# Moving stores, a split, six additions and the inverse in the second half of a fused attention and two-layer network kernel

## The chip, the cores and the metric

The kernel runs on one core of a Trainium2 chip. The metric is the device time of one execution in microseconds (us). Times of the kernel before: 1921.9 us is the median of three runs (1918.7, 1921.9, 1922.95).

## The reference

```python
def _moe2_ref(x, w_in, w_out, a, b):
    h = x @ w_in                                   # 4608 x 512 times 512 x 2048
    P = a[0] + a[1] * h + a[2] * h2 + a[3] * h3    # h2 = h*h, h3 = h2*h
    Q = 1.0 + np.abs(b[0]) * np.abs(h) + np.abs(b[1]) * h2
    g = P / (Q + 1e-06)
    return (g @ w_out).astype(np.float32)          # 2048 x 512
...
x = attention(q, k, v)            # pooled keys and values
x = _moe_ref(x, ...)              # a gated network, 512 -> 1536 -> 512
return _moe2_ref(x, ...)
```

Attention and the first network fill the first 1025 us of the span and are not touched. The change lies in the second network (`_moe2_ref`), which the kernel calls its second phase.

## The kernel before

The 4608 tokens are nine blocks of 512 (`j` = 0 to 8). The 2048 columns of `h` are cut into 16 slices of 128 (`f`), two slices make a quad pair `q` (0 to 7). Products are of float32 accuracy: every operand is split into a high part (rounded copy, ScalarE) and a low part (the rest, a subtraction), and `mm3` (L257) does three matmuls for each product.

**Stage A** (1025 to 1270 us) takes blocks 0 to 2 plainly: 24 sets `n`, one for each (j, q). Set `n` has 24 matmuls for `h` (a PSUM tile `h` with two buffers), then one or two calls of `out2()`. `out2()` is 12 matmuls that add one slice of `g @ w_out` for an earlier set into four PSUM banks `acco`. Class `Units` works on a set's `h`: on ScalarE `a_square` (squares L1123, absolute value L1124), `a_line` (L1127), `a_log` (logarithm L1131, exponential L1132). On VectorE `v_under` (L1136), `v_over` (L1140, L1141; both read PSUM) and `v_inverse` (L1145, L1146), after which `quotient` (L1152) writes `g`. The tiles `w4`, `t4` and `ln4` have two halves, used by even and odd sets in turn. In between, sets 1 to 16 prepare sums of the input weights for stage B: on odd sets `i_sums` (L1211 to L1218: two additions of 128x512, four of 128x256, on GpSimd), on even sets `i_parts` splits them (`ip`). Sets 3 to 6 and 11 to 14 split the next block's input (`z`), sets 18 to 21 do a sum of stage B's inputs on VectorE (`token_sum`), sets 20 to 23 split such a sum (`token_part2`).

**Stage B** (1270 to 1859 us) takes blocks 3 to 8 two at a time, in 24 rounds `m` (three pairs of blocks times eight q). Such a round uses seven products of 6 matmuls instead of eight (`product2`, with sums and differences of blocks), and four calls of `out2()`; 90 matmuls in all. In order on TensorE: a11, out2 number 1, s1, s2, out2 number 2, a12 and s4, s3, out2 number 3, a22, out2 number 4. After a11 ScalarE copies bank `a` into bank `b` (L1351, the mark of a round below); s1 goes to bank `c` of the same PSUM tile `hb` and so starts behind that copy. After s1 ScalarE copies `c` out (`cq`, L1354). Then unit `one` of the round goes through `Units` after s4, unit `two` after a22; the second half of unit `two` (logarithm, inverse, quotient) is done in the next round. Rounds 7, 8, 15 and 16 also split inputs of the next pair (`z`).

`next_split()` gives the two halves of the split of a finished `g` for `out2()`: `high` on ScalarE (L1175) and `low` on GpSimd (L1178), both 128x1024, into a tile `gt` with two buffers. A round makes two splits: the first behind unit `one`'s `a_line`, the second behind unit `two`'s. In the end, what is left of `out2()` runs by itself (the tail, with the low parts on VectorE).

**Block end.** When slice f = 15 of a block is done, `out2()` at once copies the four banks `acco` to tiles `ob` (L1200, ScalarE, two buffers) and stores each (L1202) by a DMA on SyncE's queue. Six block ends fall into stage B, always behind out2 number 1 of a round (rounds 1, 5, 9, 13, 17, 21), so that the copies stand on ScalarE ahead of unit two's `a_log` and of the copy L1351. One falls into stage A (set 13), two into the tail.

Of the kernel before, what the change touches and what calls it, by code (L numbers as in the profile page):

```python
# [10 lines left out]
F32 = mybir.dt.float32  # L11
F32R = mybir.dt.float32r
U32 = mybir.dt.uint32
AF = mybir.ActivationFunctionType
ALU = mybir.AluOpType
# [4 lines left out]
P = 128  # L20
# [43 lines left out]
def attention_gated_rational(  # L64
# [1041 lines left out]
    with tc.tile_pool(name="p2", bufs=1, reuse_waits="tile") as p2:  # L1106
# [43 lines left out]
        def quotient(j, q, t, e):  # L1150
            g = stash[j, q] = wslot(f"g{j}_{q}", (P, 2, BLK), F32)
            nc.vector.scalar_tensor_tensor(g, t, neg[:, 0:1], e, op0=ALU.add, op1=ALU.mult)  # L1152
# [26 lines left out]
                outs.extend(((j, 2 * q + s), gt[:, :, s, :]) for s in range(2))  # L1179
            return high, low  # L1180

        def out2():

            for fn in waiting:
                fn()
            waiting.clear()
            if not outs:
                return
            (j, f), gt = outs.pop(0)
            if f == 0:  # L1190
                accs[j] = alloc_acc(f"o{j}")
            w = o2_t.pop(0)
            for i in range(4):
                mm3(accs[j][i], [(gt, slice(i * P, (i + 1) * P), w, full)], first=f == 0, last=f == NF2 - 1)
            o2_load()
            if f == NF2 - 1:
                acc = accs.pop(j)
                for i in range(4):
                    ob = p2.tile([P, DM], F32, tag="ob", name=f"ob{j}_{i}", bufs=2)
                    nc.scalar.activation(ob, acc[i], AF.Copy)  # L1200
                    r0 = j * BLK + i * P
                    nc.sync.dma_start(out[r0 : r0 + P, :], ob)  # L1202


        sums2 = {}
# [1 line left out]
        def i_sums(k):  # L1207
            r = wslot(f"ir{k}", (P, 2, 2, QUART), F32)
            for i in range(2):
                w = W2[f"i2_{2 * k + i}"]  # L1210
                nc.gpsimd.tensor_tensor(  # L1211
                    r[:, i].rearrange("p h c -> p (h c)"), f32(w[:, 0, :]), f32(w[:, 1, :]), op=ALU.add
                )
            t = sums2[k] = wslot(f"is{k}", (P, 4, QUART), F32)
            nc.gpsimd.tensor_tensor(t[:, 0], r[:, 1, 0], r[:, 1, 1], op=ALU.add)
            nc.gpsimd.tensor_tensor(t[:, 1], t[:, 0], r[:, 0, 0], op=ALU.subtract)
            nc.gpsimd.tensor_tensor(t[:, 2], r[:, 0, 0], r[:, 1, 0], op=ALU.subtract)
            nc.gpsimd.tensor_tensor(t[:, 3], r[:, 0, 1], t[:, 1], op=ALU.subtract)  # L1218

        def i_parts(k):  # L1220
            t = sums2.pop(k)
# [65 lines left out]
        for n, (j, q) in enumerate(sets):  # L1287
            if j + 1 < PLAIN and q == 1:
                raws[j + 1] = keep.tile([P, KT, BLK], F32, tag="xraw", name=f"yraw{j + 1}")
                nc.sync.dma_start(raws[j + 1], y_dram[j + 1])  # L1290
            if j + 1 < PLAIN and q == 3:
                xs[j + 1], cv = convert_x(halves(raws.pop(j + 1)), f"z{j + 1}", True)
                xs["cv"] = cv
            if j == PLAIN - 1 and q == 1:
                raw_load(0)
            h = ps_h.tile([P, 2, BLK], F32, tag="h", name=f"h2_{j}_{q}")
            for i in range(2):
                mm3(h[:, i, :], [(W2[f"i2_{2 * q + i}"], slice(kk * P, (kk + 1) * P), xs[j][kk], full) for kk in range(KT)])
                if j == PLAIN - 1:
                    W2.pop(f"i2_{2 * q + i}")  # L1300
            u = Units(h, n % 2)
            for _ in range(1 if n % 4 else 2):
                out2()
            u.a_square()
            u.a_line()
            cut = next_split() if len(outs) < 2 else None
            if cut:
                cut[0]()
            u.v_under()
            u.v_over()  # L1310
            if cut:
                cut[1]()
            u.a_log()
            if xs.get("cv"):
                xs["cv"].pop(0)()
            u.v_inverse()
            quotient(j, q, t4[:, n % 2], w4[:, n % 2])
            k, r = divmod(n - 1, 2)
            if 0 <= k < NQ:
                (i_parts if r else i_sums)(k)  # L1320
            if 1 <= k < NQ + 1 and not r:
                i_store(k - 1)
            if j == PLAIN - 1:
                if 2 <= q < 6:
                    token_sum(0, q - 2)
                if q >= 4:
                    token_part2(0, ("b11", "t1", "t2", "b21")[q - 4])
                if q == 6:
                    stream2(0)
            if q == NQ - 1:  # L1330
                xs.pop(j)


        nm = len(PAIRS2) * NQ
        old = None
        for m in range(nm):
# [15 lines left out]
            product2(c, m, "s1", "t1", True)  # L1352
            cq = p2.tile([P, BLK], F32, tag="cq", name=f"cq2_{m}")
            nc.scalar.activation(cq, c, AF.Copy)  # L1354
            product2(a, m, "s2", "t2")
            if old:
                old[1].v_inverse()
# [18 lines left out]
            product2(a, m, "s3", "t3")  # L1376
            one.a_square()
            one.a_line()
            cut = next_split()
            if cut:  # L1380
                cut[0]()
            nc.vector.tensor_tensor(h22, cq, a, op=ALU.add)  # L1382
            one.v_under()
            one.v_over()
            if cut:
                cut[1]()
            one.a_log()
            out2()
            product2(a, m, "a22", "t4")
# [82 lines left out]
```

## Time and profile before

| what | value |
|---|---|
| median of three runs | 1921.9 us |
| the profiled execution | 1922.85 us |
| its span (first to last instruction) | 1921.1 us |
| TensorE busy, share of the span | 1761.4 us, 92% |
| VectorE busy | 1362.1 us, 71% |
| ScalarE busy | 1105.2 us, 58% |
| GpSimd busy | 578.5 us, 30% |
| mean granted TensorE clock | 0.976 of full |
| stores of the result | 36 of 256 KB |

TensorE is the engine with most work, and matmuls are pipelined, so its busy share overstates how near it is to its peak. The table averages over stages with different limits. What the change is worth has to be read stage by stage, from what each engine waits for.

### The profile page before, as it was taken

Reading aid. Unit: us, or ns where it says so; the run is one execution under the profiler, and the core shown is the slowest. Engines: PE = TensorE matmul, PEld = TensorE weight load, DVE = VectorE, ACT = ScalarE, POOL = GpSimd, SP = SyncE. Lnnn points to the kernel's source line nnn. Section 1 sums busy time; section 2 is a strip of 40 time slices with the busy share of each in tenths; the row PEclk is TensorE's granted clock in tenths of the full one; section 3 lists DMA queues with packets and bytes.
Section 4 is the critical chain, followed back from the end, with each engine's and each line's share of the span. In section 5 each row is a group of like instructions: output and inputs, shape, how many; then the busy total and the mean of one; then the engine's idle time right before and its main releaser. Section 6 shows DMA issues by size and latency. Waiting matters only on the chain.

```text
span 1921.1 us, 23468 instructions
## 1 busy us (share of the span) xinstructions
PE 1761.4 (92%) x8068; PEld 1409.6 (73%) x8068; DVE 1362.1 (71%) x1852; ACT 1105.2 (58%) x1636; POOL 578.5 (30%) x603
## 2 busy tenths in 40 slices
PE   6889999999999999999999899977989798989898
PEld 5667777777787787878887677766767676767677
DVE  7996665566777666457777999985869586957671
ACT  5685455556656655345555666665657465756562
POOL 2344545424352542200003485211212121212120
PEclk9999999999999999999999999988999899989999
DMA  7522756579998889999353244344545555454535
GB/s 253 204 98 80 235 176 212 181 254 351 364 326 293 315 312 311 346 369 316 135 197 136 105 152 167 134 163 167 194 160 186 189 171 180 165 186 164 186 121 175
DMA packets 201670, 404.80 MB, mean 211 GB/s; under 512 B 16208, under 2 KB 88528, under 8 KB 200912
## 3 DMA queue, kind: packets, MB, share of 16 engines
q1 hardware_dynamic: 200832, 402.98, 60.4%
q8 instruction: 64, 1.05, 0.2%
q14 instruction: 54, 0.44, 0.1%
q10 hardware_dynamic: 720, 0.33, 0.1%
HBM read 305.73 MB, written 97.52 MB: 210 GB/s over the span
## 4 chain that ended last, share of the span: by engine, by line
PE 41%; DVE 10%; ACT 4%; DMA 4%; POOL 3%; issue 2%; SPq 0%; POOLq 0%; ACTq 0%; DVEq 0%
PE acco L257 14%; PE hb L257 6%; PE ya L1082 5%; PE ha L257 5%; PE ca L257 4%; POOL gt L1178 3%; PE yc L1082 3%; DVE w L1136 3%; PE cc L257 2%; DMA out<-ob 2%; DVE w L1146 2%; DVE w L1145 2%; PE yb L1082 1%; DVE t L1141 1%; DVE t L1140 1%
## 5 line engine op out<-in xcount | busy, mean ns | idle before, releaser
L257 PE MATMUL acco<-wo,gt 128*128 128x512 f32 x1728 | 421.0, 392 | 26.7 <-POOL gt L1178 25.4
L257 PEld LDWEIGHTS acco<-wo,gt 128*128 128x128 f32 x1728 | 323.1, 188 | 106.2 <-POOL gt L1178 37.0
L1178 POOL TENSOR_TENSOR gt<-g,gt 128x1024 fp32r<-128x1024 f32 x63 | 157.9, 2506 | 777.2 <-ACT gt L1175 740.5
L257 PE MATMUL h<-z,wi 128*128 128x512 f32 x576 | 142.5, 405 | 18.9 <-DVE t L1141 17.5
L257 PEld LDWEIGHTS h<-z,wi 128*128 128x128 f32 x576 | 111.4, 196 | 48.6 <-issue 16.1
L1145 DVE SCALAR_TENSOR_TENSOR w<-w,ln 128x1024 f32<-128x1024 f32 x72 | 98.7, 1371 | 60.5 <-ACT ln L1132 60.5
L1131 ACT ACTIVATE ln<-w 128x1024 f32<-128x1024 f32 x72 | 76.4, 1062 | 74.5 <-DVE w L1136 74.3
L257 PE MATMUL vp<-x,wv 128*128 128x512 f32 x432 | 111.0, 404 | 5.9 <-DVE wv L150 5.9
L1136 DVE SCALAR_TENSOR_TENSOR w<-sq,neg,w 128x1024 f32<-128x1024 f32 x72 | 110.0, 1528 | 8.8 <-ACT w L1124 8.7
L257 PE MATMUL gp<-x,wg 128*128 128x512 f32 x432 | 109.4, 400 | 2.5 <-DVE wg L150 2.5
L257 PE MATMUL acc<-ht,wo 128*128 128x512 f32 x432 | 106.8, 396 | 0.0
L1123 ACT ACTIVATE sq<-hb 128x1024 f32<-128x1024 f32 x24 | 24.7, 1029 | 138.7 <-PE hb L257 138.7
L257 PEld LDWEIGHTS vp<-x,wv 128*128 128x128 f32 x432 | 80.5, 191 | 26.0 <-DVE wv L150 8.5
L257 PEld LDWEIGHTS gp<-x,wg 128*128 128x128 f32 x432 | 79.4, 188 | 23.4 <-DVE wg L150 4.7
L1175 ACT ACTIVATE gt<-g 128x1024 fp32r<-128x1024 f32 x72 | 76.5, 1063 | 34.0 <-PE acco L257 25.6
L1146 DVE SCALAR_TENSOR_TENSOR w<-w,ln 128x1024 f32<-128x1024 f32 x72 | 93.8, 1303 | 2.5
L1152 DVE SCALAR_TENSOR_TENSOR g<-t,neg,w 128x1024 f32<-128x1024 f32 x72 | 94.2, 1336 | 1.1
L257 PEld LDWEIGHTS acc<-ht,wo 128*128 128x128 f32 x432 | 80.4, 188 | 18.3
L1132 ACT ACTIVATE ln<-ln,lnb 128x1024 f32<-128x1024 f32 x72 | 83.0, 1152 | 2.3
L118 POOL TENSOR_TENSOR rawo<-rawo 128x256 uint32<-128x256 uint32 (+1 forms) x41 | 31.2, 760 | 133.0 <-DVE rawo L115 63.0
L1382 DVE TENSOR_TENSOR ha<-cq,ha 128x512 f32<-128x512 f32 x24 | 16.7, 696 | 63.9 <-PE ha L257 63.7
L257 PE MATMUL ca<-x1t,sw 128*128 128x512 f32 x216 | 57.6, 401 | 2.4 <-DVE x1t L95 2.1
(318 smaller groups left out, 4046.0 us busy)
## 6 DMA issues: line engine op xcount, KB each, us to landing
wo<-o_parts SPq DMA_DIRECT2D x144, 512.0 KB, 3.7
sw<-sd SPq DMA_DIRECT2D x72, 512.0 KB, 7.5
iw<-si SPq DMA_DIRECT2D x48, 512.0 KB, 7.6
sw<-wd SPq DMA_DIRECT2D x36, 512.0 KB, 5.8
h<-hq SPq DMA_DIRECT2D x36, 512.0 KB, 7.0
sd<-sp SPq DMA_DIRECT2D x24, 512.0 KB, 4.1
iw<-i_parts SPq DMA_DIRECT2D x24, 512.0 KB, 4.7
sw<-vd SPq DMA_DIRECT2D x36, 256.0 KB, 7.9
```

The costliest lines, as they stand in the source:

```text
L118: nc.gpsimd.tensor_tensor(tu if spare else hi_word, hi_word, lo_word, op=ALU.add)
L257: nc.tensor.matmul(acc, st[:, lw, cols], mv[:, rw, mcols], start=first and i == 0, stop=last and i == n - 1, skip_group_check=seeded,)
L1082: nc.tensor.matmul(banks[q], w[:, lw, cols], t[:, rw, :], start=opened and k == 0 and m == 0, stop=k == NK - 1 and m == 2, skip_group_chec ...
L1123: nc.scalar.activation(sq, self.h, AF.Square)
L1131: nc.scalar.activation(ln, w4[:, self.s], AF.Ln, scale=LNS, bias=C1 * LNS)
L1132: nc.scalar.activation(ln, ln, AF.Exp, scale=-1.0, bias=lnb)
L1136: nc.vector.scalar_tensor_tensor(w, sq, neg[:, 5:6], w, op0=ALU.mult, op1=ALU.add)
L1145: nc.vector.scalar_tensor_tensor(w, w, C1, ln, op0=ALU.add, op1=ALU.mult)
L1146: nc.vector.scalar_tensor_tensor(w, w, 2.0, ln, op0=ALU.subtract, op1=ALU.mult)
L1152: nc.vector.scalar_tensor_tensor(g, t, neg[:, 0:1], e, op0=ALU.add, op1=ALU.mult)
L1175: nc.scalar.activation(gt[:, 0], g, AF.Copy)
L1178: eng.tensor_tensor(gt[:, 1], g, f32(gt[:, 0]), op=ALU.subtract)
```

## The change

Four things are edited, all in the second phase.

1. *Stores.* The copies and stores at a block end move out of `out2()` into `store()`, which is put into the list `waiting` and called by the next `leave()`. `leave()` runs at the start of the next `out2()`, and in stage B also right behind the copy `cq`. There are four buffers `ob` instead of two, and the store's DMA is issued by ScalarE behind each copy, no longer by SyncE.
2. *Split.* The first of a round's two splits moves up, from behind unit one's `a_line` to right behind `cq` (and behind `leave()`). Where `g` is not there yet in the program (rounds 8 and 16), it stays at its old place.
3. *Sums.* The six additions of `i_sums` move from GpSimd to VectorE.
4. *Inverse.* In stage A `v_inverse` and `quotient` of set n are done after `v_over` of set n + 1. The set with two calls of `out2()` becomes n = 3, 7, 11, ... instead of 0, 4, 8, ...

```diff
+        def store(j, acc):
+            for i in range(4):
+                ob = p2.tile([P, DM], F32, tag="ob", name=f"ob{j}_{i}", bufs=4)
+                nc.scalar.activation(ob, acc[i], AF.Copy)
+                r0 = j * BLK + i * P
+                nc.scalar.dma_start(out[r0 : r0 + P, :], ob)
+        def leave():
             for fn in waiting:
                 fn()
             waiting.clear()
+        def out2():
+            leave()
...
             if f == NF2 - 1:
-                acc = accs.pop(j)
-                for i in range(4):
-                    ob = p2.tile([P, DM], F32, tag="ob", name=f"ob{j}_{i}", bufs=2)
-                    nc.scalar.activation(ob, acc[i], AF.Copy)
-                    r0 = j * BLK + i * P
-                    nc.sync.dma_start(out[r0 : r0 + P, :], ob)
+                waiting.append(lambda j=j, acc=accs.pop(j): store(j, acc))
...
-                nc.gpsimd.tensor_tensor(
+                nc.vector.tensor_tensor(
                     r[:, i].rearrange("p h c -> p (h c)"), f32(w[:, 0, :]), f32(w[:, 1, :]), op=ALU.add
...
-            for _ in range(1 if n % 4 else 2):
+            for _ in range(2 if n % 4 == 3 else 1):
                 out2()
...
-            u.v_inverse()
-            quotient(j, q, t4[:, n % 2], w4[:, n % 2])
+            if n:
+                behind()
+            behind = lambda u=u, j=j, q=q, n=n: (u.v_inverse(), quotient(j, q, t4[:, n % 2], w4[:, n % 2]))
...
+        behind()
...
             nc.scalar.activation(cq, c, AF.Copy)
+            leave()
+            cut = next_split()
+            if cut:
+                cut[0]()
+                cut[1]()
             product2(a, m, "s2", "t2")
...
-            cut = next_split()
-            if cut:
-                cut[0]()
+            late = None if cut else next_split()
+            if late:
+                late[0]()
```

The first place is ScalarE at the block end of round 5. `acco` are the four banks, `ob` the copies, `ln` the logarithm and exponential of unit two, `hb` the copy L1351, `gt` the high part of a split, `sq` the square of unit one. Before:

```order
L1175 ACTIVATE gt_0_11927<-g_0_11416 128x1024
L1200 ACTIVATE ob_0_11976<-acco_0_11420 128x512
L1200 ACTIVATE ob_1_11979<-acco_1_11421 128x512
L1200 ACTIVATE ob_2_11982<-acco_2_11422 128x512
L1200 ACTIVATE ob_3_11985<-acco_3_11423 128x512
L1131 ACTIVATE ln_9663<-w_9662 128x1024
L1132 ACTIVATE ln_9663<-ln_9663,lnb 128x1024
L1351 ACTIVATE hb_11990<-ha_11955 128x512
L1354 ACTIVATE cq_5_11998<-hb_11990 128x512
L1123 ACTIVATE sq<-hb_11990 128x1024
```

The same place now (the copy is line 1359, `cq` line 1362):

```order
L1359 ACTIVATE hb_11978<-ha_11955 128x512
L1362 ACTIVATE cq_5_11986<-hb_11978 128x512
L1185 ACTIVATE ob_0_11988<-acco_0_11423 128x512
L1187 DMA out<-ob_0_11988 128x512
L1185 ACTIVATE ob_1_11991<-acco_1_11424 128x512
L1187 DMA out<-ob_1_11991 128x512
L1185 ACTIVATE ob_2_11994<-acco_2_11425 128x512
L1187 DMA out<-ob_2_11994 128x512
L1185 ACTIVATE ob_3_11997<-acco_3_11426 128x512
L1187 DMA out<-ob_3_11997 128x512
L1175 ACTIVATE gt_1_12000<-g_1_11566 128x1024
L1123 ACTIVATE sq<-hb_11978 128x1024
```

The four copies moved from ahead of the copy into `hb` to behind `cq`, each now has a DMA issue behind it, and the split's high part stands ahead of the square.

The second place is VectorE in stage A, from the end of set 1 into set 2. `g_1` is the quotient of set 1, `ip` a part of the weights' sums. Before:

```order
L1141 SCALAR_TENSOR_TENSOR t_9664<-t_9664,neg,h_0_1_9718 128x1024
L1145 SCALAR_TENSOR_TENSOR w_9662<-w_9662,ln_9663 128x1024
L1146 SCALAR_TENSOR_TENSOR w_9662<-w_9662,ln_9663 128x1024
L1152 SCALAR_TENSOR_TENSOR g_1_9756<-t_9664,neg,w_9662 128x1024
L1136 SCALAR_TENSOR_TENSOR w_9662<-sq,neg,w_9662 128x1024
L1140 TENSOR_TENSOR t_9664<-t_9664,h_0_2_9766 128x1024
L1141 SCALAR_TENSOR_TENSOR t_9664<-t_9664,neg,h_0_2_9766 128x1024
```

Now, from the second addition of the sums at the end of set 1 to set 3:

```order
L1216 TENSOR_TENSOR ir_9751<-wi_1_9233 128x512
L1220 TENSOR_TENSOR is_9754<-ir_9751 128x256
L1221 TENSOR_TENSOR is_9754<-is_9754,ir_9751 128x256
L1222 TENSOR_TENSOR is_9754<-ir_9751 128x256
L1223 TENSOR_TENSOR is_9754<-ir_9751,is_9754 128x256
L1136 SCALAR_TENSOR_TENSOR w_9662<-sq,neg,w_9662 128x1024
L1140 TENSOR_TENSOR t_9664<-t_9664,h_0_2_9759 128x1024
L1141 SCALAR_TENSOR_TENSOR t_9664<-t_9664,neg,h_0_2_9759 128x1024
L1145 SCALAR_TENSOR_TENSOR w_9662<-w_9662,ln_9663 128x1024
L1146 SCALAR_TENSOR_TENSOR w_9662<-w_9662,ln_9663 128x1024
L1152 SCALAR_TENSOR_TENSOR g_1_9797<-t_9664,neg,w_9662 128x1024
L95 TENSOR_TENSOR ip_1_9800<-is_9754,ip_0_9799 128x1024
```

The sums now stand on VectorE between two sets, and the quotient that follows set 2's `v_over` is that of set 1.

## Rows read from the trace of the kernel before

**Rows 1.** Waits of TensorE, 1280 to 1922 us: total us, times, longest us.

```profile
PE hb L257 <- ACT hb L1351: 49.2, 8, 10.9
PE acco L257 <- POOL gt L1178: 23.1, 25, 1.0
```

**Rows 2.** Line 1351 as a group, and on ScalarE's timeline: start us, us, instruction [idle before].

```profile
L1351 ACT ACTIVATE hb<-ha x24: 577/582/582, 1269.8 to 1837.2; 128x512 f32<-128x512 f32 x24
...
1328.20 0.58 ACT L1351 ACTIVATE hb<-ha 128x512 f32<-128x512 f32 x1 [0.26 <-DVE t L1141]
...
1349.97 0.58 ACT L1351 ACTIVATE hb<-ha 128x512 f32<-128x512 f32 x1 [0.26 <-DVE t L1141]
```

**Rows 3.** Timeline of one round of stage B, 1320 to 1345 us.

```profile
1330.58 0.60 ACT L1354 ACTIVATE cq<-hb 128x512 f32<-128x512 f32 x1 [1.80 <-PE hb L257]
...
1331.69 2.89 PE L257 MATMUL acco<-wo,gt 128*128 128x512 f32 x12
...
1337.35 1.03 ACT L1123 ACTIVATE sq<-hb 128x1024 f32<-128x1024 f32 x1 [6.17 <-PE hb L257]
...
1341.50 2.39 POOL L1178 TENSOR_TENSOR gt<-g,gt 128x1024 fp32r<-128x1024 f32 x1 [13.25 <-ACT gt L1175]
...
1343.59 1.39 DVE L1145 SCALAR_TENSOR_TENSOR w<-w,ln 128x1024 f32<-128x1024 f32 x1 [0.44 <-ACT ln L1132]
...
1343.94 1.43 PE L257 MATMUL acco<-wo,gt 128*128 128x512 f32 x5 [0.94 <-POOL gt L1178]
```

**Rows 4.** Waits of ScalarE, 1280 to 1922 us: total us, times, longest us.

```profile
ACT ob L1200 <- DMA out<-ob: 32.3, 8, 7.7
```

**Rows 5.** Timeline at the block end of round 5, ScalarE.

```profile
1397.01 1.21 ACT L1200 ACTIVATE ob<-acco 128x512 f32<-128x512 f32 x2 [3.37 <-DMA out<-ob]
```

**Rows 6.** Busy us (and count) of PE, PEld, DVE, ACT, POOL by stretch; PEclk, DMA.

```profile
1030.00:1225.00 195.00, 177.22 (x744) 141.39 (x743) 186.77 (x132) 127.93 (x130) 109.63 (x60) 0.97 0.38 136
...
1400.25:1423.86 23.61, 22.04 (x87) 17.72 (x88) 17.37 (x16) 13.48 (x16) 4.77 (x2) 0.90 0.40 139
```

**Rows 7.** Waits of TensorE, 1020 to 1280 us.

```profile
PE h L257 <- DVE t L1141: 17.5, 12, 3.4
PE hb L257 <- ACT hb L1351: 5.4, 1, 5.4
```

**Rows 8.** VectorE's timeline in stage A: the same operation of sets 17 and 18.

```profile
1212.27 1.22 DVE L1145 SCALAR_TENSOR_TENSOR w<-w,ln 128x1024 f32<-128x1024 f32 x1
...
1219.63 1.22 DVE L1145 SCALAR_TENSOR_TENSOR w<-w,ln 128x1024 f32<-128x1024 f32 x1
```

**Rows 9.** Line 1136 in stage A: ns least/median/most, first and last start us.

```profile
L1136 DVE SCALAR_TENSOR_TENSOR w<-sq,neg,w x24: 1270/1752/3429, 1033.1 to 1265.3; 128x1024 f32<-128x1024 f32 x24
```

**Rows 10.** Timeline in stage A, set 20: GpSimd and VectorE together.

```profile
1232.08 3.24 POOL L1178 TENSOR_TENSOR gt<-g,gt 128x1024 fp32r<-128x1024 f32 x1 [12.53 <-ACT gt L1175]
...
1232.97 3.42 DVE L1136 SCALAR_TENSOR_TENSOR w<-sq,neg,w 128x1024 f32<-128x1024 f32 x1
```

**Rows 11.** VectorE's groups by shape, whole span: busy us, mean ns | idle.

```profile
L95 DVE TENSOR_TENSOR x<-pv,x 128x128 fp32r<-128x128 f32 x16 | 4.1, 287 | 1.8 <-ACT x L94 1.5
...
L95 DVE TENSOR_TENSOR z0t<-z0t,z0t 128x512 fp32r<-128x512 f32 x6 | 3.9, 684 | 0.0
```

**Rows 12.** Line 1202, the 36 stores of the result: issue to landing.

```profile
DMA to landing us min/median/max: 2.0/2.3/8.3
```

**Rows 13.** Timeline of the tail, TensorE.

```profile
1873.12 42.46 PE L257 MATMUL acco<-wo,gt 128*128 128x512 f32 x186 [0.98 <-ACT ob L1200]
```

**Rows 14.** DMA issues at the launch on ScalarE's and SyncE's timelines.

```profile
0.73 0.41 ACTq L273 DMA_DIRECT2D q<-in_q  x1
1.17 0.46 ACTq L534 DMA_DIRECT2D ident<-in_ident  x1
...
0.74 2.29 SPq L273 DMA_DIRECT2D k<-in_k  x5
```

**Rows 15.** ScalarE's groups by shape, 1028 to 1250 us: line 1124.

```profile
L1124 ACT ACTIVATE w<-h,cab 128x1024 f32<-128x1024 f32 x22 | 24.3, 1106 | 0.0
```

More of the change, by code (lines that the diff above doesn't have):

```diff
@@ L1180, in next_split @@
             return high, low
-        def out2():
+        def store(j, acc):
[5 more added lines that the diff above has]
+        def leave():
             for fn in waiting:
@@ L1214, in i_sums @@
             t = sums2[k] = wslot(f"is{k}", (P, 4, QUART), F32)
[L1215 to L1218, printed above, removed]
+            nc.vector.tensor_tensor(t[:, 0], r[:, 1, 0], r[:, 1, 1], op=ALU.add)
+            nc.vector.tensor_tensor(t[:, 1], t[:, 0], r[:, 0, 0], op=ALU.subtract)
+            nc.vector.tensor_tensor(t[:, 2], r[:, 0, 0], r[:, 1, 0], op=ALU.subtract)
+            nc.vector.tensor_tensor(t[:, 3], r[:, 0, 1], t[:, 1], op=ALU.subtract)
         def i_parts(k):
@@ L1384, in attention_gated_rational @@
             one.v_over()
-            if cut:
-                cut[1]()
+            if late:
+                late[1]()
             one.a_log()
```

## The prediction

> **What bounds the kernel now.** The change touches stage A (24 sets, 1025 to 1270 us), stage B (24 rounds, to 1859 us) and the tail, so I read TensorE's waits there first. In stage B and the tail two matter: 49.2 us in eight waits of `hb` on the copy L1351, up to 10.9 us each, and 23.1 us in 25 waits of `acco` on GpSimd's split, about 0.9 each [rows 1]. Next comes the period. The copy marks the rounds: 24 of them, first at 1269.8, last at 1837.2, so 23 rounds took 567.4 us; two undisturbed marks lie 21.77 us apart (1328.20 and 1349.97) [rows 2]. 23 such rounds are 500.7 us, and 66.7 us are extra.
>
> The timeline of a round shows its loop. TensorE's s1 waits for the copy, the copy waits 0.26 us for unit two's `v_over` on VectorE [rows 2], and that stands behind unit one's work, which began when ScalarE squared at 1337.35. On the way VectorE waits 0.44 us for the logarithm and exponential, which stand behind the split's high part on ScalarE, and its L1145 then takes 1.39 us. Beside this GpSimd starts the split only at 1341.50, and TensorE's fourth `out2()` stops 0.94 us for it [rows 3].
>
> At a block end ScalarE waits for stores to land before it has a buffer `ob`: 32.3 us in eight waits [rows 4], 3.37 us at round 5 [rows 5]. The copy L1351 stands behind, so TensorE stops too, and the round after runs at a granted clock of 0.90 and takes 23.61 us instead of 21.77 [rows 6].
>
> Stage A is another place: VectorE is busy 186.77 of 195 us [rows 6], and TensorE waits 17.5 us for its `v_over` [rows 7]. With VectorE free of GpSimd, a set's six operations take 1219.63 - 1212.27 = 7.36 us [rows 8]; from the first set's L1136 to the last's the stage took 1265.3 - 1033.1 = 232.2 us for 23 sets, 10.1 each. L1136 goes from 1.27 up to 3.43 us there [rows 9]; one of 3.42 us ends only after GpSimd's split, which started just before it, is over [rows 10].
>
> **The change part by part.** *Stores.* Of the 66.7 us extra, rounds 7, 8, 15 and 16 have input splits worth 1.3 each, 5.1 in all, which stay (two splits of 128x512 at 0.684 on VectorE [rows 11]). That leaves 61.6 us for six block ends: 47.3 of it are TensorE's six long waits (49.2 less two of 0.96), the rest is the low clock after them. With four buffers, `ob` is used again four rounds, some 85 us, later, and no store took more than 8.3 us to land [rows 12], so this wait goes. What is late next: the second `out2()` of the round starts the next block in the same four banks. The copies now stand behind `cq`, which ends at 1331.18, while that `out2()` begins at 1331.69 [rows 3] and wants its last bank nine matmuls of 0.228 (42.46 / 186 [rows 13]) later, at 1333.74. Four copies of 0.60 end at 1333.6; three DMA issues between them, at the 0.41 us of ScalarE's own [rows 14], make it 1334.9: 1.2 us per block end, 7.2 in all. The least is nothing, if the issues do not hold ScalarE. The split behind them ends by 1336.4, before the square wants ScalarE at 1337.35, so it costs nothing there. Round 0 begins behind a wait of 5.4 us of another kind [rows 7], which I leave, with a slow round after it (1.9, as 23.61 against 21.77). Off SyncE's queue the stores hold up no load of weights; no wait of TensorE on a load shows, so that is worth nothing.
>
> *Split.* Right behind `cq` ScalarE idles 6.17 us before the square [rows 3], so a high part of 1.06 fits, and GpSimd is done some 6 us before the fourth `out2()`: 0.94 goes. But TensorE then meets the copy L1351 sooner. The loop through the copy gets shorter only by VectorE's 0.44 wait and by L1145's excess over 1.22 [rows 8], 0.17, together 0.6, for the high part is no longer ahead of the logarithm; so a round takes 21.2, and a wait of 0.6 to 0.7 on the copy takes the place. That is 0.57 for 21 of 23 rounds (8 and 16 keep the old place): 12.0 us. The bounds are 0 (the copy eats it all) and 1.2 (90 matmuls of 0.228 are 20.5). GpSimd now runs beside the two quotients, which read SBUF alone, and may hold them up 2.4 us [rows 3]; in most rounds VectorE then has over 2.5 us to spare. In rounds 7 and 15 it has not: 2 x 1.5 = 3.0.
>
> Stage B: 61.6 - 7.2 - 1.9 - 3.0 + 12.0 = **61.5 us less**.
>
> *Sums and inverse* work on one engine, VectorE, and go together. Taking the sums off GpSimd ends their collisions, but adds two additions of 512 columns, 0.684 each, and four of 256, for which 0.287 (128 columns) and 0.684 [rows 11] give 0.42 between: 3.0 per odd set (2.5 to 4.1 with the ends). The inverse one set behind removes no VectorE work. It adds a wait: `w4` has two halves, so the absolute value of set n + 1 (1.11 [rows 15]) can only start when the quotient of set n - 1 is done, and L1136 of set n + 1 follows it. That is 1.25 with the hand-overs, unless other work lies in between. So from L1136 to L1136: eight odd sets 7.36 + 3.0 = 10.4, 83.2 us; eight even sets 8.6 (the weights' part fills the wait), 68.8; sets 17 to 19 and 22 8.6, 34.4; sets 20 and 21 with a sum and two splits 9.9, 19.8; eight input splits 5.5; set 0, which drops its own inverse and then waits for set 1's operands, 5.5; the block end, with four copies and issues (4.0) ahead of a square and half hidden, 2.0. GpSimd's splits start about 2.1 us after L1136, where VectorE reads PSUM, and catch the next operation for some 0.8 us; in seven sets without sums ahead, 5.6 us. Sum 224.8 us, against 232.2: **7.4 us less**. TensorE's 936 matmuls there are 213.4 us, so it does not bound.
>
> *Tail.* The split moved up gives 0.6. At its first block end the copies come behind another high part (1.06), with issues between: 1.06 + 0.6 + 3 x 0.4 = 2.9 instead of the wait of 0.98 [rows 13]. **1.3 us more**. The last four copies end as before: the issues fall into what was a wait for a store.
>
> Together 7.4 + 61.5 - 1.3 = 67.6 us. The profiled execution took 1922.85 us, 1.75 over its span; it would be 1855.2. The median is 0.95 below the profiled one: **1854 us**.
>
> **Rivals.** *The copy eats the split* (0.15): VectorE or ScalarE find other work on the loop, and a round stays at 21.77: 12 us back, 1866 us. For it: the copy already waits 0.26 us in an undisturbed round [rows 2].
>
> *Issues hold one another up* (0.08): each of ScalarE's issues waits for a whole issue of SyncE, 0.46 more, so 1.4 per block end, eight of them: 11 us, 1865 us. Against it: at the launch both queues issued at once, SyncE five in 2.29 us, 0.46 each, and ScalarE's took 0.41 and 0.46 [rows 14]. The Trainium skill, Perfetto Trace Analysis, section "DMA Instruction — HWDGE (DVE, Sync)", says that a sequencer locks the descriptor generator for its exclusive use, which would be this rival; the rows at the launch speak against a lock between these two queues.
>
> *VectorE loses in stage A* (0.12): all 15 of GpSimd's splits block an operation for 2.1 us, as in [rows 10], 31.5 instead of 5.6: 26 us back, 1880 us. For it: with the inverse behind, L1145, L1146 and L1152 stand where GpSimd starts. The Trainium skill, SBUF — State Buffer, section "Who interferes with whom", says that a VectorE instruction with two SBUF inputs and a GpSimd one that reads SBUF exclude each other for the whole instruction, whichever is first; [rows 10] agree, and by that rule the sums' move pays less the more these meet.
>
> *TensorE becomes the bound* (0.14): the issues do not hold ScalarE and the loop closes in time, so a round takes 20.5 and a block end nothing: 0.7 x 21 + 7.2 = 22 us more, 1832 us.
>
> *Slower: ScalarE is held until its store has landed* (0.03). Then three holds of h stand between the four copies at eight block ends, 24 h, less the 9.6 us that I count for issues. From h = 3.2 us on, all is lost; at 4.3, between the median of 2.3 and the longest of 8.3 [rows 12], 24 x 4.3 - 9.6 = 94 us more than my sum, 1948 us. Against it: ScalarE's second issue at the launch began 0.03 us after its first had ended, at 1.17, while no store landed in under 2.0 [rows 12, 14].
>
> **The numbers.** My forecast has 0.48, with a range of its own of 1843 to 1862. The whole range, 1834 to 1876, takes in the copy and issue rivals and most of TensorE's; it leaves out the slow ends of stage A and the held ScalarE. A difference of 0.2%, 4 us, is about what a measurement of this kernel can tell from none. Only the held ScalarE gives slower, 0.03; 0.01 for within it; 0.96 for faster.
>
> **What would show it.** Right: no wait of `ob` on stores; waits of `hb` on the copy L1359 of under 1 us, one per round, and a period near 21.2; `acco` waits on `ob` about 1 us per block end; no half clock in stage B but at its start; in stage A a new wait of L1136 on the absolute value L1124, some 1.2 us, in sets 17 to 23, and odd sets of about 10.4. Wrong: ScalarE's issues over 1 us, a period of 21.7, or the stage from first to last L1136 longer than 232 us.

## The result and the profile after

The changed kernel takes 1856.8 us (median of four runs, 1856.6 to 1859.0) beside 1922.4 for the kernel before in the same measurement (four runs, 1918.7 to 1924.0). The ratio is 0.9664, 95% interval 0.9647 to 0.9681: faster by 3.4%. The profiled execution took 1856.56 us, its span is 1854.8. The forecast was 1854.

Waits of TensorE, and the last line one of ScalarE's, in the changed kernel, 1280 to 1860 us: total us, times, longest us (before: [rows 1, 4]).

```profile
PE hb L257 <- ACT hb L1359: 12.0, 21, 3.0
PE acco L257 <- POOL gt L1178: 3.0, 3, 1.0
PE acco L257 <- ACT ob L1185: 1.6, 1, 1.6
PE acco L257 <- DVE gt L1178: 0.4, 1, 0.4
...
ACT ob L1185 <- ACT ob L1185: 9.2, 22, 0.5
```

The waits on GpSimd's split fell from 23.1 to 3.0 us, and the long waits on the copy are gone: 19 of 0.3 us are left, and two of 3.0 us at the ends of rounds 7 and 15, which also split inputs. No copy of a result waits for a store any more. What ScalarE waits for at a block end is its own issue of the copy's store.

The copy's group, and then its marks on ScalarE's timeline (before: [rows 2]).

```profile
L1359 ACT ACTIVATE hb<-ha x24: 578/582/582, 1262.1 to 1769.5; 128x512 f32<-128x512 f32 x24
```

```profile
1332.94 0.58 ACT L1359 ACTIVATE hb<-ha 128x512 f32<-128x512 f32 x1 [0.20 <-DVE t L1141]
...
1354.06 0.58 ACT L1359 ACTIVATE hb<-ha 128x512 f32<-128x512 f32 x1 [0.20 <-DVE t L1141]
...
1375.18 0.58 ACT L1359 ACTIVATE hb<-ha 128x512 f32<-128x512 f32 x1 [0.21 <-DVE t L1141]
...
1397.46 0.58 ACT L1359 ACTIVATE hb<-ha 128x512 f32<-128x512 f32 x1 [0.20 <-DVE t L1141]
```

Undisturbed rounds are 21.12 us apart (forecast 21.2), round 5 with its block end 22.28 (forecast 1.2 over). From the first mark to the last, stage B took 507.4 us instead of 567.4. The same round 5 on ScalarE's and TensorE's timelines:

```profile
1377.58 0.60 ACT L1362 ACTIVATE cq<-hb 128x512 f32<-128x512 f32 x1 [1.82 <-PE hb L257]
1378.08 0.59 ACT L1185 ACTIVATE ob<-acco 128x512 f32<-128x512 f32 x1
1378.70 0.34 ACTq L1187 DMA_DIRECT2D out<-ob  x1
...
1378.72 4.01 PE L257 MATMUL acco<-wo,gt 128*128 128x512 f32 x12
...
1379.09 0.60 ACT L1185 ACTIVATE ob<-acco 128x512 f32<-128x512 f32 x1 [0.41 <-ACT ob L1185]
1379.71 0.34 ACTq L1187 DMA_DIRECT2D out<-ob  x1
```

A copy and its issue take 1379.09 - 1378.08 = 1.01 us, and the four end 3.6 us after the first began. TensorE's second `out2()` takes 4.01 us instead of 2.89, since its banks come free one by one: from 1280 to 1860 us TensorE's weight loads (PEld) wait 13.5 us for these copies, in 27 waits. The stretches of round 0 and of round 5 (columns as in [rows 6]):

```profile
1262.10:1289.55 27.45, 23.88 (x90) 19.08 (x90) 24.58 (x25) 16.69 (x21) 4.73 (x2) 0.88 0.33 107
...
1375.00:1398.00 23.00, 22.32 (x93) 16.60 (x91) 17.86 (x17) 16.48 (x19) 5.16 (x3) 1.00 0.64 219
```

Around the block end the granted clock is full now (1.00, where the round after one had 0.90); round 0 has 0.88.

VectorE's groups in stage A (1030 to 1260 us: busy us, mean ns | idle), and then a wait of TensorE there (before: [rows 7, 9]).

```profile
L1136 DVE SCALAR_TENSOR_TENSOR w<-sq,neg,w 128x1024 f32<-128x1024 f32 x24 | 30.8, 1282 | 13.5 <-ACT w L1124 13.1
...
L1216 DVE TENSOR_TENSOR ir<-wi 128x512 f32<-128x512 f32 x16 | 10.3, 684 | 0.0
...
L1220 DVE TENSOR_TENSOR is<-ir 128x256 f32<-128x256 f32 x8 | 3.4, 425 | 0.3
```

```profile
PE h L257 <- DVE t L1141: 1.8, 2, 1.6
```

L1136 never takes over 1.29 us now (1.28 in the mean; before 1.75 in the median, up to 3.43), although 3 us of sums per odd set stand on VectorE. From the first L1136 to the last it is 1257.1 - 1031.7 = 225.4 us instead of 232.2 (forecast 224.8), and TensorE's waits for VectorE's `v_over` fell from 17.5 us to 1.8. Not all of that is gain: in the same window TensorE now waits 7.7 us for GpSimd's split instead of 2.3, and 4.5 us for the copies of the block end.

### The profile page after: what moved, and what is told of

It reads as the page before. It is cut to its first block, busy times and chain, and to the rows that moved or that the text cites. A ratio compares the mean times of both kernels' runs of the same rounds, so it can differ in the third digit from the quotient of the medians.

```text
span 1854.8 us, 23467 instructions
## 1 busy us (share of the span) xinstructions
PE 1753.2 (95%) x8068; PEld 1401.6 (76%) x8068; DVE 1378.7 (74%) x1900; ACT 1108.9 (60%) x1636; POOL 498.8 (27%) x555
## 4 chain that ended last, share of the span: by engine, by line
PE 31%; DVE 23%; ACT 5%; issue 3%; DMA 1%; ACTq 0%; POOL 0%; DVEq 0%; POOLq 0%; SPq 0%
PE acco L257 6%; PE hb L257 5%; PE ya L1082 5%; DVE t L1141 4%; PE ca L257 4%; DVE w L1136 4%; DVE t L1140 4%; DVE w L1145 3%; PE ha L257 3%; PE yc L1082 3%; DVE w L1146 3%; PE cc L257 2%; DVE g L1152 2%; PE yb L1082 1%; ACT ob L1185 1%
## 5 line engine op out<-in xcount | busy, mean ns | idle before, releaser
L257 PE MATMUL acco<-wo,gt 128*128 128x512 f32 x1728 | 428.2, 397 | 20.3 <-POOL gt L1178 10.7
L257 PE MATMUL h<-z,wi 128*128 128x512 f32 x576 | 135.7, 392 | 3.3 <-DVE t L1141 1.8
L1152 DVE SCALAR_TENSOR_TENSOR g<-t,neg,w 128x1024 f32<-128x1024 f32 x72 | 117.7, 1661 | 1.2
L1136 DVE SCALAR_TENSOR_TENSOR w<-sq,neg,w 128x1024 f32<-128x1024 f32 x72 | 92.2, 1281 | 13.6 <-ACT w L1124 13.1
L1145 DVE SCALAR_TENSOR_TENSOR w<-w,ln 128x1024 f32<-128x1024 f32 x72 | 97.1, 1349 | 0.9 <-ACT ln L1132 0.9
L1146 DVE SCALAR_TENSOR_TENSOR w<-w,ln 128x1024 f32<-128x1024 f32 x72 | 90.3, 1255 | 2.5
L1123 ACT ACTIVATE sq<-hb 128x1024 f32<-128x1024 f32 x24 | 24.6, 1027 | 100.6 <-PE hb L257 100.6
L118 POOL TENSOR_TENSOR rawo<-rawo 128x256 uint32<-128x256 uint32 (+1 forms) x41 | 31.1, 759 | 133.3 <-DVE rawo L115 73.7
L916 ACT ACTIVATE cq<-cc 128x512 f32<-128x512 f32 x36 | 21.5, 596 | 65.1 <-PE cc L257 65.1
```

The lines of the kernel that those rows point to most:

```text
L257: nc.tensor.matmul(acc, st[:, lw, cols], mv[:, rw, mcols], start=first and i == 0, stop=last and i == n - 1, skip_group_check=seeded,)
L1136: nc.vector.scalar_tensor_tensor(w, sq, neg[:, 5:6], w, op0=ALU.mult, op1=ALU.add)
L1145: nc.vector.scalar_tensor_tensor(w, w, C1, ln, op0=ALU.add, op1=ALU.mult)
L1146: nc.vector.scalar_tensor_tensor(w, w, 2.0, ln, op0=ALU.subtract, op1=ALU.mult)
```

## The experiments

All times are medians; each ratio is to the kernel before, run beside it, with its 95% interval. "Stage A" is from the first L1136 to the 24th, "stage B" from the first mark to the last.

**One edit at a time: the stores**

```diff
+                ob = p2.tile([P, DM], F32, tag="ob", name=f"ob{j}_{i}", bufs=4)
+                nc.scalar.activation(ob, acc[i], AF.Copy)
...
+                nc.scalar.dma_start(out[r0 : r0 + P, :], ob)
...
-                    ob = p2.tile([P, DM], F32, tag="ob", name=f"ob{j}_{i}", bufs=2)
...
-                    nc.sync.dma_start(out[r0 : r0 + P, :], ob)
+                waiting.append(lambda j=j, acc=accs.pop(j): store(j, acc))
...
             nc.scalar.activation(cq, c, AF.Copy)
+            leave()
```

> The kernel before with the stores' edit alone (copies behind cq, four buffers, issued by ScalarE). Theory (each edit is worth what its own place shows): the six block ends of stage B lose 61.6 us less 1.2 each that stays and 1.9 at round 0, the tail gives 1.9 back: about 50 us less, 1872 us, undisturbed rounds still 21.77, ScalarE no longer waits for stores. Rival (the parts need one another, since a round has to close its loop): well under 40 us less.

Measured: 1871.85 us, ratio 0.9737 (0.9723 to 0.9752). Undisturbed rounds stay at 21.77, block ends are 22.95; TensorE still waits 25 times for GpSimd's split. The stores alone are worth 50 us of the 66, and they need none of the other edits.

**The split alone**

```diff
             nc.scalar.activation(cq, c, AF.Copy)
+            cut = next_split()
+            if cut:
+                cut[0]()
+                cut[1]()
...
-            cut = next_split()
-            if cut:
-                cut[0]()
+            late = None if cut else next_split()
+            if late:
+                late[0]()
```

> The kernel before with the earlier split alone. Theory: undisturbed rounds go from 21.77 to 21.1 or 21.2, block ends stay as before, so 11 to 13 us less, 1910 us. Rival (the copy into hb takes all of it back): rounds of 21.7, 1920 us or more.

Measured: 1915.33 us, ratio 0.9958 (0.9944 to 0.9972). Undisturbed rounds are 21.1, as expected. The gain is 6.8 us, where 11 to 13 had been expected: the six rounds with a block end got 3.0 us longer in all, and ScalarE waits 38.7 us in nine for stores, before 32.3 in eight [rows 4]. What the split gives is had in full only where no store is in the way.

**The sums alone, the inverse alone, and the two together**

```diff
-                nc.gpsimd.tensor_tensor(
+                nc.vector.tensor_tensor(
```

> The kernel before with the six additions on VectorE alone. Theory: 24 us more work on VectorE against some 19 us of collisions with GpSimd's additions that end, the collisions with the 15 splits stay: from first to last L1136 of stage A 232 to 240 us, so 0 to 8 us more, about 1927 us. Rival (the sums' move is what gains in stage A): 5 to 10 us less, 1914 us.

Measured: 1933.5 us, ratio 1.0057 (1.0036 to 1.0078), 11 us more, where 5 had been expected; stage A 243.8 us. The timeline shows why, at the end of set 1, and below it the group of the 16 larger additions (window 1030 to 1280 us):

```profile
1047.49 1.28 DVE L1211 TENSOR_TENSOR ir<-wi 128x512 f32<-128x512 f32 x2
...
1048.75 2.40 POOL L1178 TENSOR_TENSOR gt<-g,gt 128x1024 fp32r<-128x1024 f32 x1 [4.97 <-ACT gt L1175]
...
1048.81 2.61 DVE L1215 TENSOR_TENSOR is<-ir 128x256 f32<-128x256 f32 x1
1051.46 0.42 DVE L1216 TENSOR_TENSOR is<-is,ir 128x256 f32<-128x256 f32 x1
```

```profile
L1211 DVE TENSOR_TENSOR ir<-wi 128x512 f32<-128x512 f32 x16 | 21.3, 1375 | 0.0
```

The quotient of the set has just released its split. GpSimd starts at 1048.75, 0.06 us ahead of an addition of 0.42 us on VectorE, which then takes 2.61 us and ends 0.27 us after the split. In five of the other seven odd sets it is the additions of 512 columns that meet the split: two of them take 3.50 us instead of 1.29, and the 16 take 1.375 us in the mean instead of 0.684. The Trainium skill, SBUF — State Buffer, section "Who interferes with whom", says that a VectorE instruction with two SBUF inputs contends with a GpSimd one that reads SBUF, and that the order of issue decides which of the two blocks; these rows agree.

```diff
-            for _ in range(1 if n % 4 else 2):
+            for _ in range(2 if n % 4 == 3 else 1):
...
-            u.v_inverse()
-            quotient(j, q, t4[:, n % 2], w4[:, n % 2])
+            if n:
+                behind()
+            behind = lambda u=u, j=j, q=q, n=n: (u.v_inverse(), quotient(j, q, t4[:, n % 2], w4[:, n % 2]))
```

> The kernel before with the inverse and quotient one set behind (and two calls of out2 in sets 3, 7, ...) alone. Theory: no work leaves VectorE, GpSimd's additions still collide, and the new wait of L1136 on ScalarE's absolute value (1.25) is open in odd sets: 0 to 8 us more, about 1926 us. Rival (the inverse behind is what gains in stage A): 5 to 10 us less, 1914 us.

Measured: 1925.15 us, ratio 1.0013 (1.0003 to 1.0024), stage A 234.3. These 3 us are little more than a measurement of this kernel can tell from none. The collisions of L1136 are all but gone (1.75 us at most, before 3.43), and the new wait has come instead, uncovered: `DVE w L1136 <- ACT w L1124` 22.0 us in 12, where the kernel before has 8.7 in one. Then both, without the stores and the split:

> The kernel before with the weights' sums on VectorE and the inverse one set behind together, and neither the stores nor the early split. Theory (the two pay only together: alone the sums cost 11.4 and the inverse 3.1, because the inverse's two VectorE operations stood in the way of the additions and the additions meet GpSimd's split when the inverse doesn't stand ahead): stage A becomes that of the changed kernel, 225.4 us, less the 2.5 that the stores' edit adds there, so 223 to 226 against 232.2; stage B is that of the kernel before with round 0 about 1 to 4 us longer. Ratio 0.995 to 0.998, about 1915. Rival (they add up): 1922 + 11.4 + 3.1 = 1936, ratio 1.007, stage A about 246.

Measured: 1916.56 us, ratio 0.9977 (0.9966 to 0.9987), stage A 225.0. Alone they cost 11 and 3 us, together they save 4 to 6 (by the ratio and by the medians). The groups of this kernel in stage A:

```profile
L1136 DVE SCALAR_TENSOR_TENSOR w<-sq,neg,w 128x1024 f32<-128x1024 f32 x25 | 32.0, 1281 | 12.8 <-ACT w L1124 12.3
L1211 DVE TENSOR_TENSOR ir<-wi 128x512 f32<-128x512 f32 x16 | 10.3, 684 | 0.0
```

The additions are at their 684 ns, and the wait for the absolute value is 12.3 us instead of 22.0 (some 8.5 of either ahead of the first set): the sums fill it. From the other side, the changed kernel with its sums back on GpSimd:

```diff
-                nc.vector.tensor_tensor(
+                nc.gpsimd.tensor_tensor(
```

> The changed kernel with the six additions on GpSimd again. Theory: VectorE has 24 us less work, but collides with some 70 us of GpSimd's additions, now right where its operations on SBUF alone stand, and the wait on the absolute value is open in the odd sets: stage A from first to last L1136 about 229 to 240 us against 225.4, so 4 to 14 us more than the changed kernel, 1866 us. Rival (with the inverse behind the additions on GpSimd are hidden): 1850 us or less.

Measured: 1866.49 us, ratio 0.9718 (0.9704 to 0.9733), stage A 235.0; the wait is 22.7 us in 12, and L1145 takes 1.63 us in the mean. So each of the two edits supplies what the other lacks. The other place of the second `out2()` call came with the inverse in each of these kernels, and its share was not taken apart.

**Which part of the stores' edit does it: buffers, place or queue**

Four buffers in the kernel before, nothing else:

```diff
-                    ob = p2.tile([P, DM], F32, tag="ob", name=f"ob{j}_{i}", bufs=2)
+                    ob = p2.tile([P, DM], F32, tag="ob", name=f"ob{j}_{i}", bufs=4)
```

> The kernel before with four buffers ob and nothing else. Theory: the 32 us of ScalarE's waits for stores go and most of the low clock, but the copies, 2.5 us, still stand ahead of the logarithm and of the copy into hb, so a wait of some 3 us is left at each block end: 35 to 45 us less, about 1882 us. Rival (the buffers are all of it): 50 us or more less, 1872 us. Rival (the place is all of it): under 15 us less.

Measured: 1886.7 us, ratio 0.9821 (0.9805 to 0.9837). One number, `2` to `4`, brings 34 us. No copy waits for a store, but four copies still stand ahead of the copy into `hb`: TensorE waits 21.7 us in eight for it, a block-end round is 25.3 us and the next 23.4. The place behind `cq`, with ScalarE's queue, is worth the remaining 15 or so.

Two buffers in the changed kernel:

```diff
-                ob = p2.tile([P, DM], F32, tag="ob", name=f"ob{j}_{i}", bufs=4)
+                ob = p2.tile([P, DM], F32, tag="ob", name=f"ob{j}_{i}", bufs=2)
```

> The changed kernel with two buffers ob instead of four. Theory (the landing is the wait that the buffers took away): the third copy waits 2 to 8 us for the first store, the second out2 of the round stands behind it, and the clock falls after it: 4 to 7 us per block end, 30 to 50 us more, about 1895 us. Rival (the place of the copies is what matters, not the buffers): under 10 us more, 1862 us.

Measured: 1877.87 us, ratio 0.9776 (0.9757 to 0.9796), between theory and rival. Rounds 1 and 9 take 29 us, the other block ends 22.9 to 23.1. In round 1 the third copy waits 5.57 us:

```profile
1296.69 0.34 ACTq L1187 DMA_DIRECT2D out<-ob  x1
1302.22 0.60 ACT L1185 ACTIVATE ob<-acco 128x512 f32<-128x512 f32 x1 [5.57 <-DMA out<-ob]
```

In these two rounds SyncE issues the loads of the next pair's tokens (2 MB). Whether that delays the stores was tried by moving those loads and the sums on them by one round:

```diff
-            if p + 1 < len(PAIRS2) and q == 1:
+            if p + 1 < len(PAIRS2) and q == 2:
                 raw_load(p + 1)
...
-            if p + 1 < len(PAIRS2) and 2 <= q < 6:
-                token_sum(p + 1, q - 2)
+            if p + 1 < len(PAIRS2) and 3 <= q < 7:
+                token_sum(p + 1, q - 3)
```

> The changed kernel with two buffers for the results, and the loads of the next pair's tokens (and the token sums after them) one round later, so that they no longer fall into the round in which a block ends. Theory (a store that is issued beside those loads lands late, and the third copy of that block end waits for it): rounds 1 and 9 fall from 29 us to about 23, the longest wait of ScalarE for a store from 5.6 to about 2 us, and the time from 1877.9 to about 1866. Rival (the place of rounds 1 and 9 in the pair is the cause, not the loads): both stay at 29 and the time stays at 1878 within 2 us. A third outcome, the cost of the loads moves with them into rounds 2 and 10: those become longer than 22 us.

Measured: 1864.56 us, ratio 0.9695 (0.9680 to 0.9711). Rounds 1 and 9 are 22.9 us, rounds 2 and 10 stay at 21.1, and the third copy waits 1.02 us. The first line here is the kernel with two buffers, the second the one with the loads moved (all of ScalarE's waits for a buffer, 1280 to 1860 us):

```profile
ACT ob L1185 <- DMA out<-ob: 19.1, 13, 5.6
```
```profile
ACT ob L1185 <- DMA out<-ob: 12.0, 14, 1.5
```

The longest time from issue to landing fell with it, from 6.5 to 3.2 us. So a store lands late when it is issued beside those loads. (The sums were moved too; that they delay a store was not tried by itself, and a sum on VectorE is no transfer.) Four buffers hide this, and more: with two buffers and the loads moved the copies still wait 12.0 us in all, and the kernel is 6 to 8 us behind the changed one.

The queue: the changed kernel with its stores issued by SyncE again.

```diff
-                nc.scalar.dma_start(out[r0 : r0 + P, :], ob)
+                nc.sync.dma_start(out[r0 : r0 + P, :], ob)
```

> The changed kernel with the stores issued by SyncE again (four buffers, copies behind cq as changed). Theory (what is left of a block end, 1.17 us, is the time in which ScalarE issues between the copies): rounds with a block end go from 22.27 to 21.2, the tail gains some 1 us too, 7 to 9 us less than the changed kernel, about 1848 us. Rival (SyncE's queue matters: stores wait there ahead of loads of weights, or the loads ahead of the stores): TensorE waits for loads, 1857 us or more.

Measured: **1846.15 us**, ratio 0.9619 (0.9603 to 0.9634), 10.6 us faster than the changed kernel by the medians, 8.6 by the two ratios. At the block end of round 5:

```profile
1372.62 2.07 ACT L1185 ACTIVATE ob<-acco 128x512 f32<-128x512 f32 x4
...
1373.24 1.83 SPq L1187 DMA_DIRECT2D out<-ob  x4
...
1373.27 3.06 PE L257 MATMUL acco<-wo,gt 128*128 128x512 f32 x12
```

Four copies take 2.07 us instead of the 3.6 above with their issues, SyncE issues them beside, and the block-end round falls from 22.28 to 21.30 us. Of 10.4 us between the two traces, the six block ends of stage B give 5.7, round 0 gives 1.7 and the tail 3.0; 2.8 lie ahead of stage B, 1.4 of them in the part that was not edited; and rounds 8 and 16 take 2.9 back, by the clock (below). One part of the change, the move to ScalarE's queue, was a loss. The Trainium skill, DMA: Bandwidth & Descriptors, section "Issuing engines are not separate DMA queues", says that issuing from several engines saves only the time of the sequencer, usually small beside the transfer. Here the transfer is hidden (2.0 us in the median to landing from ScalarE's queue, 2.3 from SyncE's, and no copy waits for it). What costs is the 0.34 us of the issue, since the next copy starts only after it: copies 1.01 us apart instead of 0.5.

**A version that goes on from there**

```diff
-                nc.scalar.dma_start(out[r0 : r0 + P, :], ob)
+                nc.sync.dma_start(out[r0 : r0 + P, :], ob)
...
-            u.a_log()
+            if n < len(sets) - 1:
+                u.a_log()
...
-                if q >= 4:
+                if 4 <= q < 7:
...
-        behind()
...
             nc.scalar.activation(b, a, AF.Copy)
+            if not m:
+                u.a_log()
+                token_part2(0, "b21")
...
             nc.vector.tensor_tensor(h22, cq, a, op=ALU.add)
+            if not m:
+                behind()
...
         while turn2 or outs:
+            leave()
```

> The changed kernel with the stores issued by SyncE (1846.2 us), and two places mended. Round 0: the logarithms and the token part b21 of the last set of stage A run behind the copy of round 0 (L1359) instead of ahead of it, and its inverse and quotient behind the addition of L1395 instead of ahead of that of L1371. Tail: the four copies of a block's results run ahead of the next split instead of behind it. Theory (round 0 is long because ScalarE's logarithms and VectorE's inverse of set 23 stand ahead of what TensorE waits for): the wait on the copy falls from 3.8 to under 1.5 us and that on L1371 from 1.9 to nothing, of which later VectorE work takes back 1 to 2; the tail's wait on the copies falls from 1.6 to about 0.6; together 3 to 5 us, so 1841 to 1843, ratio 0.959 to 0.960. Rival (VectorE is full in round 0 and keeps its length whatever the order): round 0 stays within 1 us of 25.7, only the tail's 1 us is had, 1845.

Measured: **1843.79 us**, ratio 0.9592 (0.9580 to 0.9605), the fastest here; its interval overlaps that of the version before it, so the times alone do not show a gain over that one. In the traces the tail is 2.0 us shorter (80.3 from 82.3, with no wait for the copies). Round 0 went as the rival said. Its copy waits 1.81 us for set 23's L1141 on VectorE, which still reads the buffer of `h`, so TensorE's wait on it fell only from 3.8 to 2.6; the wait on L1371 is gone. But rounds 0 and 1 together took 25.48 + 22.71 us, before 25.73 + 21.30. VectorE is busy 25.2 of the 25.5 us of round 0 there (24.6 of 25.7 before). Round 1 begins behind a wait of 2.29 us for the copy, before 0.32, and its granted clock is 0.92, before 1.00. So what was put off in round 0 comes back in round 1. What stage B gained lies in round 8 (21.8 from 24.7), where this version changes nothing. To the edit itself go the 2.0 us of the tail, less the 1.2 that rounds 0 and 1 lost.

Rounds 8 and 16 vary with the granted clock. In six of the kernels here that have both the moved stores and the early split, each begins behind a wait of 3.0 to 3.1 us for the copy (of rounds 7 and 15). Where the granted clock was 1.00 over the first 8 us of the round, it took 21.8 us; where it was 0.79, 23.2 to 23.5; where it was 0.57, 24.7. With the stores alone that wait is 1.0 us, and the clock stayed at 1.00. Why the clock falls after this wait one time and not the next stays open.

## Why the prediction was right, and where a term was off

*What bounded the kernel*: shown. Long stops at block ends came from ScalarE standing still for store buffers; four buffers alone remove 34 us.

*Stores*: forecast 61.6 - 7.2 - 1.9 = 52.5 us in stage B; the edit alone gave 567.4 - 513.7 = 53.7 there. The 1.2 us per block end is 1.16 measured. It shows as a longer `out2()` (4.01 us) and not, as the signs had it, as a wait of `acco` on `ob`. The working took 0.41 for an issue; the trace has 0.338, and a copy with its issue 1.01, as 0.60 + 0.41:

```profile
L1187 ACTq DMA_DIRECT2D out<-ob x36: 338/338/353, 1175.8 to 1851.7; - x36
...
DMA to landing us min/median/max: 2.0/2.0/6.3
```

*Split*: the loop through the copy closes at 21.1 instead of 21.2, with a wait of 0.32 on the copy instead of 0.6 to 0.7. The rival in which the copy eats the gain is out, and so is the one in which TensorE becomes the bound (20.5). Two of the signs did not come: at the ends of rounds 7 and 15 the wait on the copy is 3.03 us, not under 1, and behind the first of them the granted clock was low outside the start of stage B as well (0.79 over the first 8 us of round 8). With the stores alone that wait is 1.00 us and the clock stays full. The length of rounds 7 and 15 was in the sum, the low clock behind them was not.

*Round 0, the mis-sized term*: I wrote "Round 0 begins behind a wait of 5.4 us of another kind, which I leave, with a slow round after it (1.9, as 23.61 against 21.77)". The round took 27.45 us, 6.3 over. The timeline of it:

```profile
1262.77 2.87 PE L257 MATMUL hb<-z0t,iw 128*128 128x512 f32 x6 [3.93 <-ACT hb L1359]
1265.43 1.95 PE L257 MATMUL ha<-z0t,iw 128*128 128x512 f32 x6
...
1267.36 2.51 POOL L1178 TENSOR_TENSOR gt<-g,gt 128x1024 fp32r<-128x1024 f32 x1 [5.86 <-ACT gt L1175]
...
1267.62 3.33 DVE L1146 SCALAR_TENSOR_TENSOR w<-w,ln 128x1024 f32<-128x1024 f32 x1
1271.06 1.28 DVE L1152 SCALAR_TENSOR_TENSOR g<-t,neg,w 128x1024 f32<-128x1024 f32 x1
1272.27 0.69 DVE L1371 TENSOR_TENSOR hb<-cq,ha 128x512 f32<-128x512 f32 x1
...
1273.01 4.61 PE L257 MATMUL hb<-z0b,iw 128*128 128x512 f32 x12 [2.90 <-DVE hb L1371]
```

The wait ahead of the round is there (3.93 us) with slow matmuls behind it, 2.87 and 1.95 us where round 5 has 1.67 and 1.55: 1.6 us, about the 1.9 counted. Not counted was a second wait, 2.90 us for the addition L1371, and the slow matmuls behind that, 4.61 us where round 5 has 2.92: 4.6 us together. The inverse that is left over from set 23 runs at the start of round 0, and the early split of that round meets it: L1146 starts 0.26 us after GpSimd and takes 3.33 us, and L1371 stands behind. Two of the runs bear this out: with the split moved but the inverse not, TensorE has no such wait in round 0; with sums and inverse but the split not moved, L1146 takes 1.23 us and the wait is 0.69. I had counted the inverse as moved within stage A, and not what its last one is put in front of.

*Rounds 7, 8, 15 and 16*: 23.90, 23.44, 23.90 and 21.83 us. The forecast has 24.0 for 7 and 15. In rounds 8 and 16 the old split place keeps its wait on GpSimd, about 1 us, as written. Together stage B gave 60.0 us where 61.5 was forecast: round 0 cost 4.4 more, the other rounds gave 2.9 of it back. That the forecast came so near (1854, measured 1856.8) is in part luck: these errors cancel.

*Sums and inverse*: forecast 7.4 less, from the first L1136 to the last; measured 6.8. Part of this is no gain: one inverse with its quotient, some 3.7 us, is merely carried over the end of that stretch (22 inverses in it instead of 23), and is paid for behind it. The two edits by themselves saved 4 to 6 us. The reason given, that the two go together, is shown by the three runs above. The new wait of L1136 on the absolute value was forecast for sets 17 to 23, some 1.2 us each; of these it came in set 18 alone (1.19), besides set 1 (1.78) and set 15, behind the block end (1.32). (The fourth of the four waits, 8.8 us, stands ahead of the first set.) The stretch from set 17 to set 23 took 56.2 us all the same, where 54.2 was counted. The rival in which VectorE loses stage A is out: the splits now fall mostly beside L1140 and L1141, which read PSUM, and L1136, L1140, L1141, L1146 and L1152 stand at their least; L1145 alone has about 4 us over (31.1 for 22 against 1.22 each), where 5.6 was counted.

*Tail*: 1.4 us more (85.3 from 83.9), forecast 1.3; the wait on the copies is 1.63, before 0.98 [rows 13], where 2.9 had been taken.

*Issues hold one another up*, and *ScalarE held until landing*: neither happened. The second is out: a copy follows the one before in 1.01 us, and a store needs 2.0 to land. The first was hardly put to the test: the 36 issues lie between 338 and 353 ns, but only one of them (1293.09, 0.34 us) overlaps an issue of SyncE (1292.92, 0.33 us), and neither was longer for it. The Trainium skill, Perfetto Trace Analysis, section "DMA Instruction — HWDGE (DVE, Sync)", says that the generator is locked for exclusive use; a wait for a lock is not to be seen in this one overlap, and more no row here can tell.

## What to carry to other kernels

Before a store or an issue is given to a compute engine's queue, look what stands behind it on that engine: 36 issues of 0.34 us cost some 9 to 11 us in all here, while with SyncE issuing them TensorE waited for no load. Buffers for results pay when a copy's wait for them stands ahead of something that TensorE needs; where a wait for a landing varies, look which large load is issued in the same round. And try edits that share an engine together before dropping one: here one that loses alone (11 us) and one that gains nothing alone win some 5 us together, since one fills the wait that the other opens. And when work is moved past the end of a stage, count it where it lands: the inverse carried into round 0 met the early split there, and the round took 27.45 us, with the stores alone 24.47.

## What the runs showed of the hardware that was not expected

A small VectorE operation can cost as much as a large one: an addition of 0.42 us took 2.61, because GpSimd's split had started 0.06 us earlier. A store of 256 KB lands after 2.0 us in the median, but beside 2 MB of loads a copy stood 5.57 us for one; with the loads a round later it stood 1.02, and the rounds that took the loads stayed at 21.1 us. And an issue on ScalarE costs more than its own 0.34 us: with the hand-over, copies stand 1.01 us apart instead of 0.5. Last, a wait of TensorE of 3.0 us was followed by a low clock in some executions and not in others, and the round behind it took from 21.8 to 24.7 us.
